# Writing out the prologue's order for every engine, three transpositions for k's maximum, and idle products in TensorE's waits

## The chip, the cores and the metric

The kernel runs on one core of a Trainium2 chip. The metric is the device time of one execution in microseconds (us), lower is better; 854.16 us is the median of three runs before the change. A core has a matrix engine (TensorE; PE in the rows, and PEld for its weight loads), a vector engine (VectorE, DVE), an activation engine (ScalarE, ACT), a general one (GpSimd, POOL) and a queue that issues the transfers (SyncE, SP). Each works through its own list of instructions in order and waits on semaphores for the others.

## The reference, cut to what matters

A linear attention (q softmaxed along the head dimension, k along the sequence), then two MLPs over all 2304 tokens, all in float32:

```python
# q, k, v: (4, 8, 576, 64)
q_s = exp(q - max(q, axis=-1)); q_s /= sum(q_s, axis=-1) + 1e-9
k_s = exp(k - max(k, axis=2));  k_s /= sum(k_s, axis=2) + 1e-9
kv  = einsum('bhsd,bhse->bhde', k_s, v)
x   = einsum('bhsd,bhde->bhse', q_s, kv)     # -> (2304, 512)
h   = x @ w_in;  x2  = (h - tanh(h)) @ w_out          # d_ff 2048
h2  = x2 @ w2_in; out = (max(h2,0) + log1p(exp(-|h2|))) @ w2_out
```

The inputs arrive as float64 bits; the kernel takes the float32 parts of the weights out of them itself.

## The kernel before

The 2304 tokens are cut into five blocks (512, 256, 512, 512, 512). For each block and each of four head pairs `hp`, `kv_task` makes the kv matrix of a batch and `x_task` makes the attention's output x, transposed, split into a high and a low float32r part (`xh`, `xl`). For each block and each of 16 steps `f`, `hidden` makes a tile h of the hidden layer with 12 products of 128x512, `gate` makes h - tanh(h) and splits it into `gh` and `gl`, and `mid_out` adds 12 products to the four output tiles x. The products of step n stand behind `hidden` of step n + 2. The second MLP follows when the first is done.

The weights come as 64-bit words. `w_task(p)` loads two steps' worth, and `convert` and `parts` turn each into a high and a low part: an ACT pass into `top` (L137), a DVE pass that joins it with the lower bits (L139), an ACT cast (L147, the high part), a DVE subtraction (L148, the low part). A tile i then holds the parts of w_in, a tile o those of w_out.

The prologue is the work before the first `hidden`: batch 0's four `kv_task`, block 0's four `x_task` and `w_task(0)`. Each is a generator. A string `order` says whose next part is recorded; a part holds the work of several engines, and a scheduler then sets each engine's list. For one k: the load; a maximum over the six rows of each partition in three DVE passes (L281 to L283, tile m); a transposition on TensorE (pm, L290); its maximum (mx, L292); a second transposition that spreads it over the partitions (pb, L295); the subtraction (L297); the exponential on ACT (L298); 12 products with v (pk, L305), two to a pair of rows, which use half of the array each; the reciprocal of the sum (r, L309 and L310); two scaled copies into kv (L313). For one q: the maximum (qm, L342), the subtraction on POOL (L344), the exponential (L345), the sum and its reciprocal (qsum, L348 to L350), the scaling on POOL (qn, L352), four transpositions (pt, L363), a copy (qs, L383), the product with kv (px, L388), and xh (L390) and xl (L391). The products of float32 tiles show as two rows each, the transpositions as one.

The eight PSUM banks have tags: two `h`, four `acc`, two `a`. The list `wide` hands the banks to the prologue's 20 tiles, from its end; its first entry, h0, goes to the last tile, px of head pair 3, and the first `hidden` needs h0 too.

All loads are issued by SP: k of all four head pairs, then q, then v, then the weights.

Of the kernel before, what the change touches and what calls it, by code (L numbers as in the profile page):

```python
# [9 lines left out]
F32 = mybir.dt.float32  # L10
# [11 lines left out]
def linear_attention_two_mlps(  # L22
# [32 lines left out]
    P = 128  # L55
# [62 lines left out]

    turn = itertools.count()

    def convert(raw, tops=None):

        words = raw.rearrange("p (f two) -> p f two", two=2)
        low, n = words[:, :, 0], words.shape[1]
        h3 = raw.bitcast(BF16).rearrange("p (f four) -> p f four", four=4)[:, :, 2]
        if tops:  # L130
            at_ = next(turn)
            top = tops[at_ % 2] if n > DM else tops[at_ // 2 % 2][:, at_ % 2 * DM :][:, :n]
        else:
# [9 lines left out]
        return f32(low)  # L143

# [12 lines left out]
    def w_task(p):  # L157
# [3 lines left out]
        for w, at_, pool_of in (("i", IN_AT, in_pool), ("o", OUT_AT, lambda _: weights_out)):  # L161
# [13 lines left out]
        yield  # L175
        yield
        if p:
            yield
            yield
        made = []  # L180
        for w, pool in (("i", in_pool(p)), ("o", weights_out)):
            made.append(pool.tile([P, 2, 2, DM], F32R, tag=f"{w}{p}", name=f"{w}0_{f}"))
        for k in range(2):
            wi[f + k] = tuple(made[0][:, n, k].rearrange("p (c f) -> p c f", c=NC) for n in range(2))
            wo[0, f + k] = tuple(made[1][:, n, k] for n in range(2))
        for k in range(2):

            for n, (t, raw) in enumerate(zip(made, raws)):
                if len(raw) == 2:
                    parts([part[:, k] for part in (t[:, 0], t[:, 1])], convert(raw[k], tops))  # L190
                elif k == n:
                    parts([part.rearrange("p k f -> p (k f)") for part in (t[:, 0], t[:, 1])], convert(raw[0], tops))
            yield
# [63 lines left out]
    def kv_task(b, hp, pool, bufs, lag=False):  # L257
# [15 lines left out]
        nc.gpsimd.memset(vt[:, :, :, D:], 1.0)  # L273
        m1 = pool.tile([KP, 2, D], F32, tag="m1", name=f"m1{nm}", bufs=bufs)
        if pool is att:

            m3 = vt[:, : KJ // 2, :, :D].rearrange("p j h d -> p h j d")
        else:
            load_v(vt)
            m3 = pool.tile([KP, 2, KJ // 2, D], F32, tag="m3", name=f"m3{nm}", bufs=2)  # L280
        nc.vector.tensor_tensor(m3, kt[:, :, : KJ // 2], kt[:, :, KJ // 2 :], op=ALU.max)  # L281
        nc.vector.tensor_tensor(m1, m3[:, :, 0], m3[:, :, 1], op=ALU.max)
        nc.vector.tensor_tensor(m1, m1, m3[:, :, 2], op=ALU.max)  # L283
        if pool is att:
            load_v(vt)
        yield
# [16 lines left out]
        for j in range(KJ):  # L303
            for h in range(2):
                nc.tensor.matmul(  # L305
                    pk[h * D : (h + 1) * D, : D + 2], kt[:, h, j], vt[:, j, h], start=j == 0, stop=j == KJ - 1
                )
        r = pool.tile([P, 1], F32, tag="r", name=f"r{nm}", bufs=bufs)
        nc.vector.tensor_scalar(r, pk[:, D : D + 1], 1e-9, None, op0=ALU.add)  # L309
        nc.vector.reciprocal(r, r)  # L310
        for h in range(2):
            d = slice(h * D, (h + 1) * D)
            nc.scalar.mul(kv[b % 2, hp][d, d], pk[d, :D], r[d])  # L313
# [8 lines left out]
    def x_task(i, hp, pool, bufs, lag=False):  # L322
# [39 lines left out]
        for j in range(J):  # L362
            nc.tensor.transpose(pt[:, j * P : (j + 1) * P], qn[:, j].rearrange("p h d -> p (h d)"), ident)  # L363
        if i == NB - 1:

# [15 lines left out]
        else:  # L381
# [206 lines left out]
    def advance():  # L588
        for t in list(running):
            if next(t, "end") == "end":  # L590
                running.remove(t)
# [39 lines left out]
    tasks |= {f"x{hp}": x_task(0, hp, pro, NHP) for hp in range(NHP)}  # L631
    tasks["w"] = w_task(0)
    order = """k0 k1 k2 k3 x0 x1 x2 x3 k0 k1 k2 k3 w k0 k1 k2 k3 x0 k0 x1 k1 x2 k2 x3 k3 x0 k0 x1 k1 x2 k2 x3 k3 x0 x1 w w x2 x3 x0 x1 x2 x3 w w"""
    for n, name in enumerate(order.split()):
        next(tasks[name], None)
        if n == 7:
            constants()
    assert all(next(t, None) is None for t in tasks.values())
    pro_stack.close()
# [7 lines left out]
    for n in range(min(starts), NB * NF - 2):  # L647
# [128 lines left out]
```

## Time and profile before

| | before |
|---|---|
| median of 3 runs (851.07 to 855.46) | 854.16 us |
| the profiled execution | 854.06 us, span 852.2 us |
| PE busy | 827.4 us, 97% |
| DVE, ACT, POOL busy | 496.4, 396.9, 28.2 us |
| chain that ended last, by engine | PE 82%, DMA 7%, DVE 5%, ACT 3% |

The profile is of one execution, and its span runs from the first to the last instruction; the execution's time is 1.9 us longer. PE's busy time counts a product from its start to its modelled end, so neighbours overlap. An idle time is put down to the instruction that ended it last. The column PEclk is the granted clock as a share of 2.4 GHz where the trace holds a record of it, and 1.00 where it holds none; the first record lies at 24.3 us.

### The profile page before, as it was taken

To read this page: it belongs to the slowest core of one execution; us is meant where nothing else is said; L and a number is where in the kernel's file an instruction comes from. 1 tells how busy PE (TensorE), PEld (TensorE's weight loads), DVE (VectorE), ACT (ScalarE), POOL (GpSimd) and SP (SyncE) were. 2 spreads that over 40 slices of the span, in tenths; PEclk is the share of its full clock that TensorE was granted. 3 is DMA by queue.
4 is the path that set the end of the run, shared out by engine and by line. 5 is a ranking of instruction groups with operands and counts; after the bars stand their busy time and mean duration, and the time that the engine had idled before them with its cause. 6 is when DMAs were issued, how large, how long until landed. Compare 5 with 4: busy or idle time off the path is not lost.

```text
span 852.2 us, 11605 instructions
## 1 busy us (share of the span) xinstructions
PE 827.4 (97%) x4348; PEld 711.2 (83%) x4348; DVE 496.4 (58%) x860; ACT 396.9 (47%) x628; POOL 28.2 (3%) x46
## 2 busy tenths in 40 slices
PE   4899999999999999999999999999999999999998
PEld 3677788987888888888888898899898898988986
DVE  7598998888764344444786543456633454634433
ACT  3796766566643232323756432344432443423322
POOL 5000000000000000010010000011000010000000
PEclk9899999999999999999999999999999999999999
DMA  9948677667710010022462644346544444544422
GB/s 253 318 152 253 207 234 263 200 200 250 243 58 13 11 51 13 13 74 70 165 243 89 200 115 126 112 120 197 185 124 112 117 121 121 186 124 111 116 58 75
DMA packets 86904, 121.32 MB, mean 142 GB/s; under 512 B 24640, under 2 KB 51264, under 8 KB 86848
## 3 DMA queue, kind: packets, MB, share of 16 engines
q1 hardware_dynamic: 86848, 120.57, 46.0%
q8 instruction: 35, 0.57, 0.3%
q14 instruction: 21, 0.17, 0.1%
HBM read 96.43 MB, written 24.12 MB: 141 GB/s over the span
## 4 chain that ended last, share of the span: by engine, by line
PE 82%; DMA 7%; DVE 5%; ACT 3%; issue 1%; SPq 1%; POOL 0%; ACTq 0%; DVEq 0%
PE h L406 17%; PE one L501 12%; PE o L572 8%; PE o L573 8%; PE o L571 8%; PE x L433 6%; PE x L434 6%; PE x L435 6%; PE seven L501 6%; DMA rawi<-in_moe_w_in_dram 4%; PE two L501 3%; PE px L388 1%; DMA x2d<-x2s 1%; PE pk L305 1%; PE pt L363 1%
## 5 line engine op out<-in xcount | busy, mean ns | idle before, releaser
L406 PE MATMUL h<-xh,i 128*128 128x512 f32 (+1 forms) x640 | 200.2, 379 | 3.5 <-DVE xl L391 3.5
L406 PEld LDWEIGHTS h<-xh,i 128*128 128x128 f32 x640 | 118.2, 190 | 25.3 <-DVE xl L391 4.3
L433 PE MATMUL x<-gh,o 128*128 128x512 f32 (+1 forms) x320 | 118.1, 369 | 2.2 <-DVE x2s L442 1.3
L406 PE MATMUL h<-xl,i 128*128 128x512 f32 (+1 forms) x320 | 119.0, 372 | 0.0
L434 PE MATMUL x<-gl,o 128*128 128x512 f32 (+1 forms) x320 | 118.0, 369 | 0.0
L435 PE MATMUL x<-gh,o 128*128 128x512 f32 (+1 forms) x320 | 117.9, 368 | 0.0
L501 PE MATMUL one<-xf,wf 128*128 128x384 f32 x576 | 116.8, 337 | 0.4 <-ACT u L516 0.4
L572 PE MATMUL o<-o,gh 128*128 128x512 f32 x288 | 113.7, 395 | 0.0
L573 PE MATMUL o<-o,gh 128*128 128x512 f32 x288 | 113.7, 395 | 0.0
L571 PE MATMUL o<-o,gl 128*128 128x512 f32 x288 | 112.3, 390 | 0.0
L501 PEld LDWEIGHTS one<-xf,wf 128*128 128x128 f32 x576 | 103.1, 188 | 7.0 <-ACT u L516 0.8
L416 DVE TENSOR_TENSOR g<-h,g 128x512 f32<-128x512 f32 (+1 forms) x80 | 50.6, 634 | 66.0 <-ACT g L415 65.8
L415 ACT ACTIVATE g<-h 128x512 f32<-128x512 f32 (+1 forms) x80 | 45.3, 566 | 85.7 <-PE h L406 85.4
L516 ACT COPY u<-one 128x384 f32<-128x384 f32 x72 | 34.4, 478 | 107.7 <-PE one L501 107.7
L521 DVE TENSOR_TENSOR hh<-seven,u 128x384 f32<-128x384 f32 x48 | 26.6, 554 | 86.0 <-ACT u L516 86.0
L433 PEld LDWEIGHTS x<-gh,o 128*128 128x128 f32 x320 | 60.3, 189 | 12.7 <-DVE x2s L442 1.5
L406 PEld LDWEIGHTS h<-xl,i 128*128 128x128 f32 x320 | 61.1, 191 | 9.5
L434 PEld LDWEIGHTS x<-gl,o 128*128 128x128 f32 x320 | 60.4, 189 | 9.8
L435 PEld LDWEIGHTS x<-gh,o 128*128 128x128 f32 x320 | 60.3, 189 | 9.9
L417 ACT CAST gh<-g 128x512 fp32r<-128x512 f32 (+1 forms) x80 | 46.6, 582 | 44.2 <-DVE g L416 44.1
L418 DVE TENSOR_TENSOR gl<-g,gh 128x512 fp32r<-128x512 f32 (+1 forms) x80 | 51.1, 639 | 25.1 <-ACT gh L417 24.4
L573 PEld LDWEIGHTS o<-o,gh 128*128 128x128 f32 x288 | 54.0, 187 | 11.9
(100 smaller groups left out, 1106.5 us busy)
## 6 DMA issues: line engine op xcount, KB each, us to landing
wf<-forms SPq DMA_DIRECT2D x168, 256.0 KB, 2.7
rawo<-in_moe_w_out_dram SPq DMA_DIRECT2D x32, 511.8 KB, 5.1
rawi<-in_moe_w_in_dram SPq DMA_DIRECT2D x32, 511.0 KB, 5.5
forms<-stage SPq DMA_DIRECT2D x24, 512.0 KB, 3.0
k<-in_k_dram SPq DMA_DIRECT2D x16, 288.0 KB, 3.9
v<-in_v_dram SPq DMA_DIRECT2D x32, 144.0 KB, 3.4
out_dram<-ot SPq DMA_DIRECT2D x18, 256.0 KB, 2.7
x2d<-x2s SPq DMA_DIRECT2D x16, 256.0 KB, 2.4
```

The costliest lines, as they stand in the source:

```text
L406: nc.tensor.matmul(p, w[:, c], x[:, c, :n], start=at == 0, stop=at == 3 * NC - 1)
L415: tanh[0] = nc.scalar.activation(g, h, AF.Tanh)
L416: nc.vector.tensor_tensor(g, h, g, op=ALU.subtract)
L417: nc.scalar.copy(gh, g)
L418: nc.vector.tensor_tensor(gl, g, f32(gh), op=ALU.subtract)
L433: nc.tensor.matmul(a, ol[:, s], gh, start=first, stop=False)
L434: nc.tensor.matmul(a, oh[:, s], gl, start=False, stop=False)
L435: nc.tensor.matmul(a, oh[:, s], gh, start=False, stop=last)
L501: nc.tensor.matmul(a, w[:, wp, c], x[:, xp, c], start=first and at == 0, stop=at == 5, skip_group_check=True)
L571: nc.tensor.matmul(a, gl[:, c], oh, start=first, stop=False)
L572: nc.tensor.matmul(a, gh[:, c], ol, start=False, stop=False)
L573: nc.tensor.matmul(a, gh[:, c], oh, start=False, stop=last)
```

## The change

1. The parts of the tasks are cut finer (`yield FINE`). Outside the prologue `advance` runs over the fine cuts, so the parts there stay as they were. `convert` and `parts` are joined into `steps_of`, which stops between its four passes; `w_task(0)` goes by them, first both halves of w_in, then both of w_out (before: w_in and w_out of the first half, then of the second).
2. A new string `order` names every fine part, and `in_order` makes each recorded instruction follow the one before it on its engine, so that the recorded order is the engine's order. What follows the prologue on ACT and DVE is held behind the prologue's last instruction on either.
3. The loads of q stand between those of k, and v of head pair 0 ahead of k of head pair 3.
4. In the prologue the three DVE passes for k's maximum become one (L299: 6 rows to 3); three transpositions (L314) and a maximum over 288 columns (L317, before 96) do the rest. Later k tasks keep the three passes.
5. A number in `order` stands for so many products of the identity with itself (128 columns, float32) into a bank that nobody reads (`idle`, in the bank of h1): 32 in all, six groups of 4 and one of 8, and two of the fours stand next to each other.
6. `wide` hands h0 to px of head pair 0 and to pk of head pair 3, h1 to none, and the last tile, px of head pair 3, gets an `acc` bank.

```diff
-    def convert(raw, tops=None):
+    def steps_of(raw, out=None, tops=None):
...
         nc.scalar.activation(upper, h3, AF.Copy, scale=2.0)
+        yield FINE
...
+        if out:
+            yield FINE
+            nc.scalar.copy(out[0], f32(low))
+            yield FINE
+            nc.vector.tensor_tensor(out[1], f32(low), f32(out[0]), op=ALU.subtract)
...
+        if p == 0:
+            for t, raw in zip(made, raws):
+                for k in range(2):
+                    yield from steps_of(raw[k], [part[:, k] for part in (t[:, 0], t[:, 1])], tops)
+                    yield FINE
+            return
...
-        nc.vector.tensor_tensor(m3, kt[:, :, : KJ // 2], kt[:, :, KJ // 2 :], op=ALU.max)
-        nc.vector.tensor_tensor(m1, m3[:, :, 0], m3[:, :, 1], op=ALU.max)
-        nc.vector.tensor_tensor(m1, m1, m3[:, :, 2], op=ALU.max)
+        nc.vector.tensor_tensor(
+            m3.rearrange("p j h d -> p h j d"), kt[:, :, : KJ // 2], kt[:, :, KJ // 2 :], op=ALU.max
+        )
         if pool is att:
+            nc.vector.tensor_tensor(m1, m3[:, 0], m3[:, 1], op=ALU.max)
+            nc.vector.tensor_tensor(m1, m1, m3[:, 2], op=ALU.max)
...
+            most = [m1]
+        else:
+            most = [m3[:, j] for j in range(KJ // 2)]
...
-        nc.tensor.transpose(pm[:, :KP], m1.rearrange("p h d -> p (h d)"), ident[:KP, :KP])
+        for j, of in enumerate(most):
+            nc.tensor.transpose(pm[:, j * KP : (j + 1) * KP], of.rearrange("p h d -> p (h d)"), ident[:KP, :KP])
+        yield FINE
         mx = pool.tile([P, 1], F32, tag="mx", name=f"mx{nm}", bufs=bufs)
-        nc.vector.tensor_reduce(mx, pm[:, :KP], axis=AX, op=ALU.max)
+        nc.vector.tensor_reduce(mx, pm[:, : len(most) * KP], axis=AX, op=ALU.max)
...
-    wide += ["h0", "acc", "a", "acc", "h1", "acc", "a", "acc"] * 2 + ["h0", "acc", "a", "acc"]
+    wide += ["acc", "a", "acc", "h0", "acc", "a", "acc"] * 2 + ["acc", "a", "acc", "acc", "a", "acc"]
...
+    def in_order():
...
+        for ins in traced[start:]:
+            if ins.engine in newest:
+                tc.add_manual_dep(ins, newest[ins.engine].name, ...)
+            newest[ins.engine] = ins
...
+            for _ in range(int(name)):
+                nc.tensor.matmul(idle[:, :P], ident, ident, start=True, stop=True)
...
-    order = """k0 k1 k2 k3 x0 x1 x2 x3 k0 k1 k2 k3 w k0 k1 k2 k3 x0 k0 x1 k1 x2 k2 x3 k3 x0 k0 x1 ... w w"""
+    order = """k0 q0 k1 q1 k2 q2 k0 k3 q3 k1 k2 k3 w k0 k0 q0 4 k0 q0 k1 k0 q0 k0 k1 k1 k0 q1 k1 8 k2 ... w w w w"""
+    behind = [newest[nc.scalar.engine], newest[nc.vector.engine]]
+    with tc.issue_after(behind[0]), tc.issue_after(behind[1]):
...
-            advance()
+            for ins in behind:
+                early.enter_context(tc.issue_after(ins))
+            advance()
```

How the change moves rows, at three places. The names are those of the tiles, with the head pair or step behind them. First the head of PE's list, before:

```order
L290 MATMUL pm_0_180<-ident,m_0_139 128x96
L290 MATMUL pm_1_184<-ident,m_1_148 128x96
L290 MATMUL pm_2_188<-ident,m_2_157 128x96
L290 MATMUL pm_3_192<-ident,m_3_166 128x96
L295 MATMUL pb_0_200<-ident,mx_0_182 96x128
L295 MATMUL pb_1_208<-ident,mx_1_186 96x128
L295 MATMUL pb_2_216<-ident,mx_2_190 96x128
L295 MATMUL pb_3_224<-ident,mx_3_194 96x128
L305 MATMUL pk_0_234<-v_0_137,k_0_99 64x66 x12
```

and after:

```order
L314 MATMUL pm_0_163<-ident,m_0_161 128x96 x3
L695 MATMUL idle<-ident 128x128 x4
L320 MATMUL pb_0_178<-ident,mx_0_173 96x128
L314 MATMUL pm_1_182<-ident,m_1_176 128x96 x3
L320 MATMUL pb_1_191<-ident,mx_1_186 96x128
L695 MATMUL idle<-ident 128x128 x8
L314 MATMUL pm_2_209<-ident,m_2_201 128x96 x3
L332 MATMUL pk_0_213<-v_0_112,k_0_100 64x66 x12
L320 MATMUL pb_2_239<-ident,mx_2_232 96x128
```

One head pair's maximum now runs to its spreading (pb) before the next one starts, with three transpositions each, and the first 12 idle products stand between them.

The end of the prologue on PE, before:

```order
L363 MATMUL pt_2_348<-ident,qn_2_280 128x128 x4
L363 MATMUL pt_3_355<-ident,qn_3_304 128x128 x2
L305 MATMUL pk_3_306<-v_3_164,k_3_105 64x66 x11
L363 MATMUL pt_3_355<-ident,qn_3_304 128x128 x2
L388 MATMUL px_0_362<-qs_0_329,kv_121 128x512
L388 MATMUL px_1_366<-qs_1_336,kv_123 128x512
L388 MATMUL px_2_370<-qs_2_353,kv_125 128x512
L388 MATMUL px_3_374<-qs_3_360,kv_127 128x512
L406 MATMUL h_0_421<-xh_97,i_0_338 128x512
L406 MATMUL h_0_421<-xl_98,i_0_338 128x512
```

and after:

```order
L695 MATMUL idle<-ident 128x128 x8
L395 MATMUL pt_2_341<-ident,qn_2_335 128x128 x4
L421 MATMUL px_1_351<-qs_1_328,kv_126 128x512
L332 MATMUL pk_3_355<-v_3_150,k_3_116 64x66 x12
L421 MATMUL px_2_372<-qs_2_353,kv_128 128x512
L395 MATMUL pt_3_379<-ident,qn_3_369 128x128 x4
L695 MATMUL idle<-ident 128x128 x4
L421 MATMUL px_3_394<-qs_3_391,kv_130 128x512
L695 MATMUL idle<-ident 128x128 x4
L441 MATMUL h_0_450<-xh_97,i_0_337 128x512
```

The products px of head pairs 1 and 2 now stand ahead of the transpositions of head pair 3, and 16 idle products stand in this piece, the last four between px of head pair 3 and the first product of h_0.

ACT from the last xh to the first tanh (L415, after: L450), before:

```order
L137 ACTIVATE top_93<-rawi_1_174 128x512
L137 ACTIVATE top_92<-rawo_0_177 128x512
L390 ACTIVATE xh_97<-px_3_374 128x512
L137 ACTIVATE top_93<-rawo_0_177 128x512
L147 CAST o_0_339<-rawo_0_177 128x512
L147 CAST i_0_338<-rawi_1_174 128x512
L137 ACTIVATE top_92<-rawi_2_396 128x512
L147 CAST o_0_339<-rawo_0_177 128x512
L137 ACTIVATE top_92<-rawi_3_397 128x512
L415 ACTIVATE g_0_434<-h_0_421 128x512
```

and after:

```order
L424 ACTIVATE xh_97<-px_2_372 128x512
L424 ACTIVATE xh_97<-px_3_394 128x512
L138 ACTIVATE top_92<-rawi_1_155 128x512
L147 CAST i_0_337<-rawi_1_155 128x512
L138 ACTIVATE top_93<-rawo_0_158 128x512 x2
L138 ACTIVATE top_92<-rawi_2_425 128x512
L147 CAST o_0_338<-rawo_0_158 128x512 x2
L147 CAST i_2_438<-rawi_2_425 128x512
L450 ACTIVATE g_0_463<-h_0_450 128x512
```

Before, the passes of `w_task(0)` began ahead of the last xh, and a pass of the next pair of steps (rawi_3) stood ahead of the tanh; now every pass of `w_task(0)` but the first tile's, and both of rawi_2's, stand between the last xh and the tanh, and rawi_3's stands behind it.

## Rows read from the trace of the kernel before

**Rows 1.** Waits of PE from 32.3 us to the end: total us, times, longest:

```profile
PE h L406 <- DVE xl L391: 3.5, 1, 3.5
...
PE pm L290 <- DVE m L283: 1.3, 2, 0.8
```

**Rows 2.** Timeline of PE: start us, us, what, [idle before and releaser]:

```profile
19.10 1.58 PE L305 MATMUL pk<-v,k 96*64 96x66 f32 x22
...
21.86 2.18 PE L363 MATMUL pt<-ident,qn 128*128 128x128 f32 x9
23.97 1.06 PE L305 MATMUL pk<-v,k 96*64 96x66 f32 x22
...
25.23 3.60 PE L388 MATMUL px<-qs,kv 128*128 128x512 f32 x8
32.33 0.80 PE L406 MATMUL h<-xh,i 128*128 128x512 f32 x1 [3.49 <-DVE xl L391]
...
34.62 1.06 PE L406 MATMUL h<-xh,i 128*128 128x512 f32 x2
...
35.90 1.06 PE L406 MATMUL h<-xh,i 128*128 128x512 f32 x2
...
38.94 0.61 PE L406 MATMUL h<-xh,i 128*128 128x512 f32 x2
...
39.62 0.61 PE L406 MATMUL h<-xh,i 128*128 128x512 f32 x2
...
43.24 0.39 PE L433 MATMUL x<-gh,o 128*128 128x512 f32 x1
```

**Rows 3.** Stretches of 2 us: busy us (and count) by engine, PEclk, DMA share, GB/s:

```profile
30.00:32.00 2.00, 0.00 (x0) 0.00 (x0) 1.68 (x4) 2.00 (x5) 0.00 (x0) 0.78 0.85 230
...
34.00:36.00 2.00, 2.00 (x6) 1.54 (x6) 1.88 (x4) 1.49 (x3) 0.00 (x0) 0.50 1.01 405
```

**Rows 4.** Timeline of DVE:

```profile
4.12 0.56 DVE L281 TENSOR_TENSOR m<-k 96x384 f32<-96x384 f32 x1 [4.12 <-DMA k<-in_k_dram]
...
10.16 0.74 DVE L292 TENSOR_REDUCE mx<-pm 128x1 f32<-128x96 f32 x4
10.95 1.81 DVE L297 TENSOR_TENSOR k<-k,pb 96x768 f32<-96x768 f32 x2
...
15.59 0.67 DVE L348 TENSOR_REDUCE qsum<-q 128x8 f32<-128x512 f32 x1
...
18.56 0.97 DVE L349 TENSOR_SCALAR qsum<-qsum 128x8 f32<-128x8 f32 x2
...
31.59 0.68 DVE L391 SCALAR_TENSOR_TENSOR xl<-px,xh 128x512 fp32r<-128x512 f32 x1
...
38.48 0.69 DVE L416 TENSOR_TENSOR g<-h,g 128x512 f32<-128x512 f32 x1 [2.60 <-ACT g L415]
```

**Rows 5.** Timeline of POOL:

```profile
17.39 2.04 POOL L352 TENSOR_TENSOR qn<-q,qsum 128x512 f32<-128x512 f32 x2 [1.45 <-DVE r L309]
```

**Rows 6.** Timeline of ACT:

```profile
30.18 0.77 ACT L137 ACTIVATE top<-rawo 128x512 f16<-128x512 bf16 x1
...
31.89 0.66 ACT L147 CAST o<-rawo 128x512 fp32r<-128x512 f32 x1
...
37.85 0.60 ACT L415 ACTIVATE g<-h 128x512 f32<-128x512 f32 x1 [2.36 <-PE h L406]
```

**Rows 7.** Line L111 between 13.5 and 14.3 us: its issues and their landing:

```profile
L111 SPq DMA_DIRECT2D rawi<-in_moe_w_in_dram x2: 623/672/722, 13.2 to 13.9; - x2
...
DMA to landing us min/median/max: 5.3/5.7/6.1
```

**Rows 8.** Stretches of 10 us, columns as in rows 3:

```profile
40.00:50.00 10.00, 10.00 (x46) 8.29 (x45) 8.97 (x12) 8.94 (x12) 0.00 (x0) 1.00 0.74 263
50.00:60.00 10.00, 10.00 (x45) 8.27 (x45) 9.44 (x11) 8.81 (x11) 0.00 (x0) 1.00 0.50 162
60.00:70.00 10.00, 9.51 (x63) 7.33 (x62) 9.90 (x20) 8.02 (x10) 0.12 (x1) 1.00 0.41 120
```

More of the change, by code (lines that the diff above doesn't have):

```diff
@@ L1 @@
 import itertools
-from contextlib import ExitStack
+from contextlib import ExitStack, contextmanager
 import concourse.bass as bass
@@ L142, in convert @@
             nc.vector.scalar_tensor_tensor(low, top, 0xFFFF0000, low, op0=ALU.bitwise_and, op1=ALU.bitwise_or)
-        return f32(low)
+        if out:
[3 more added lines that the diff above has]
+            nc.vector.tensor_tensor(out[1], f32(low), f32(out[0]), op=ALU.subtract)
+    def convert(raw, out=None, tops=None):
+        for _ in steps_of(raw, out, tops):
+            pass
+        return f32(raw.rearrange("p (f two) -> p f two", two=2)[:, :, 0])
     def parts(out, x):
@@ L174, in w_task @@
                     load_out(each[k], w1_out, f + k)
-        yield
-        yield
         if p:
-            yield
-            yield
+            for _ in range(4):
+                yield
+        else:
+            yield FINE
         made = []
@@ L189, in w_task @@
                 if len(raw) == 2:
[L190 removed]
+                    convert(raw[k], [part[:, k] for part in (t[:, 0], t[:, 1])], tops)
                 elif k == n:
[L192 removed]
+                    convert(raw[0], [part.rearrange("p k f -> p (k f)") for part in (t[:, 0], t[:, 1])], tops)
             yield
@@ L589, in advance @@
         for t in list(running):
-            if next(t, "end") == "end":
+            at_ = FINE
+            while at_ == FINE:
+                at_ = next(t, "end")
+            if at_ == "end":
                 running.remove(t)
@@ L628, in linear_attention_two_mlps @@
     x_tiles(0)
-    wide += ["h0", "acc", "a", "acc", "h1", "acc", "a", "acc"] * 2 + ["h0", "acc", "a", "acc"]
+    wide += ["acc", "a", "acc", "h0", "acc", "a", "acc"] * 2 + ["acc", "a", "acc", "acc", "a", "acc"]
     tasks = {f"k{hp}": kv_task(0, hp, pro, NHP) for hp in range(NHP)}
-    tasks |= {f"x{hp}": x_task(0, hp, pro, NHP) for hp in range(NHP)}
+    tasks |= {f"q{hp}": x_task(0, hp, pro, NHP) for hp in range(NHP)}
     tasks["w"] = w_task(0)
-    order = """k0 k1 k2 k3 x0 x1 x2 x3 k0 k1 k2 k3 w k0 k1 k2 k3 x0 k0 x1 k1 x2 k2 x3 k3 x0 k0 x1 k1 x2 k2 x3 k3 x0 x1 w w x2 x3 x0 x1 x2 x3 w w"""
@@ L634, in linear_attention_two_mlps @@
-    for n, name in enumerate(order.split()):
[L635 to L638, printed above, removed]
+    idle = ps.tile([P, 512], F32, tag="h1", name="idle", bufs=1)
+    newest = {}
+    @contextmanager
+    def in_order():
+        traced = nc.cur_bb.bb.instructions
+        begin = traced[-1] if len(traced) else None
+        yield
+        start = next((n + 1 for n in reversed(range(len(traced))) if traced[n] is begin), 0)
+        for ins in traced[start:]:
+            if ins.engine in newest:
+                tc.add_manual_dep(
+                    ins,
+                    newest[ins.engine].name,
+                    mybir.DependencyInfo(mybir.DependencyClass.NoSync, mybir.DependencyReason.DATA),
+                    reason="in_order",
+                )
+            newest[ins.engine] = ins
@@ new lines, in take @@
+    def take(name):
+        if name.isdigit():
+            for _ in range(int(name)):
+                nc.tensor.matmul(idle[:, :P], ident, ident, start=True, stop=True)
+        else:
+            next(tasks[name], None)
+    order = """k0 q0 k1 q1 k2 q2 k0 k3 q3 k1 k2 k3 w k0 k0 q0 4 k0 q0 k1 k0 q0 k0 k1 k1 k0 q1 k1 8 k2 q1 q2 k1 q1
+        q2 k2 k0 q0 q2 k1 k2 q0 k0 k2 q3 k0 q0 k2 q3 q0 k1 k3 k2 q1 q0 q3 k3 k2 q0 k1 q1 k3 k1 4 k2 q2 q1 k2
+        k3 4 q1 k3 4 q2 w q0 q2 k3 q3 q1 q2 k3 w q3 q1 q2 k3 w q1 q3 4 k3 w q3 q2 q3 4 q3 q2 q3 w w w w"""
@@ L639, in linear_attention_two_mlps @@
+    for n, name in enumerate(order.split()):
+        with in_order():
+            take(name)
+            if n == 7:
+                constants()
+    behind = [newest[nc.scalar.engine], newest[nc.vector.engine]]
+    with tc.issue_after(behind[0]), tc.issue_after(behind[1]):
+        for t in tasks.values():
+            assert all(at_ == FINE for at_ in t)
     pro_stack.close()
@@ L656, in linear_attention_two_mlps @@
             x_tiles(blk + 1)
-        advance()
+        with ExitStack() as early:
+            if n < 0:
+                for ins in behind:
+                    early.enter_context(tc.issue_after(ins))
+            advance()
         while n >= -2 and len(gated) < min(n + 3, len(steps)):
```

20 lines of the change are left out of this document (17 added, 3 removed).

## The prediction

> **What bounds the kernel now.** I read the page's busy times first (PE 97% of the span), then PE's waits, its timeline over the first 45 us, and the other engines' timelines there. After 32.3 us PE hardly stops: [rows 1] show that the wait for xl, 3.5 us, ends at the first `hidden`, and that the only other waits of the first MLP's early part are two on DVE, 1.3 us together. So what comes before 32.33 us [rows 2] is nearly pure head: an earlier first `hidden` moves the whole chain, as long as DVE and ACT follow. They have little to spare: from 40 to 70 us DVE is busy 8.97 to 9.90 of each 10 us and ACT 8.02 to 8.94 [rows 8].
>
> The second cost is the clock. The steps of the same 22 rows of pk take 1.58 us at 19.1 us and 1.06 us at 24.0 us, though the column shows 1.00 for both [rows 2]: the prologue starts at the lower level (1.2 GHz) and PE rises after it has worked almost without a break from 18.5 us on. Then it waits 3.49 us for xl, and the granted clock is 0.78 and 0.50 [rows 3]: three products of `hidden` take 1.28 us (34.62 to 35.90) and later 0.68 us (38.94 to 39.62) [rows 2], 0.427 and 0.227 us each. The 36 products of h_0 to h_2 take 10.91 us from 32.33 to 43.24; at 0.227 they would take 8.17. The lost clock costs 2.7 us.
>
> **What the change costs, part by part.** I laid the new lists side by side and gave each row the step that its form has in the trace, each starting when its engine is free and its inputs are there.
>
> *Prices.* Three DVE passes of k's maximum become the first of them, 0.56 us [rows 4]. The maximum over 288 columns is not in the trace: four over 96 take 0.74 us, near 0.17 each, one over 512 some 0.60 (0.67 with its tail) [rows 4]; 288 lies between, and I take 0.36. Three transpositions cost 0.16 each at the lower level (9 of 128 columns take 2.18 with the last one's tail, 0.22 a step, three quarters of that), 0.08 at the upper. An idle product is not in the trace either. px is a float32 product of 512 columns: eight rows, two to a product, 3.60 us at the upper level, 0.43 a row and 0.86 a product [rows 2]; a quarter of the columns is 0.215, and 0.43 at the lower level. The other bound is the transposition, 0.11 to 0.22. I take the product's price: 32 of them are 6.9 us at the upper level, 13.7 at the lower, 3.5 at the least.
>
> *Loads.* k of head pair 0 stays first in SP's list, and its maximum starts at 4.12 [rows 4]. k of head pair 1 stands one load later (some 1.2 us) and is needed only behind the first subtraction. k of head pair 3, the most delayed, has about 4 us to spare by my walk. The first two weights keep their place behind the same bytes: they land near 18.5 and 20.0 us (issued at 13.2 and 13.9, 5.3 and 6.1 us on the way [rows 7]); the walk uses them at 20.3 and 27.3. The load order is at nothing; were q's bytes to hold k of head pair 1 beyond 8 us, each us would be one on the path.
>
> *The walk, first half (lower clock).* m_0 at 4.1, pm_0 4.7, four idle products until 6.9, pb_0, subtraction 7.4 to 8.3 (0.87 each by the two in 1.81 [rows 4]), mx_1 to 8.65, pb_1 8.9, eight idle products from 9.1 to 12.5, pm_2 to 13.0, pk_0 to 14.35, so r_0 on DVE at 14.6. The eight hold pm_2 back by some 2 us: m_2 is ready at 10.2. From 9.1 us on PE has no gap, so I let its clock rise between 12.5 and 16 us.
>
> *Second half (upper clock).* DVE now runs without a break: r_0 0.3, qm_3 0.6, subtraction 0.87, m_3 0.5, qsum_1 with its two small passes 1.05, r_1 0.3, mx_3 0.36, r_2 0.3, qsum_2 1.05, which is 5.3 us, and 0.3 for a wait explained next: 20.2. qn_2 on POOL takes 1.0 (two in 2.04 [rows 5]): 21.3, where the eight idle products end as well. PE then does pt_2 0.43, px_1 0.86, pk_3 0.70, px_2 0.86, pt_3 0.43, to 24.7. The next four idle products (0.86) lie under the copy qs_3; px_3 ends at 26.5; four more until 27.4, then h_0. Those four cost nothing, since h_1 needs the second half of w_in, split at 30.1; without that cover they would cost 0.86.
>
> The wait: at 18.56 two small passes of DVE take 0.97 us together, and end with POOL's second scaling (two from 17.39, 2.04 long, to 19.43) [rows 4, 5]. A DVE pass with an input from SBUF alone stood there until POOL was done. In the new order m_1 and m_3 start beside a POOL subtraction, about 0.5 and 0.3 us. By the Trainium skill, GPSIMD Engine Reference, section 8, Key points, GpSimd shares its SBUF interfaces with VectorE and contends with passes that read two SBUF inputs or run in a 2-port mode; the trace agrees with its one case of 0.8 us, and if every such pass in the prologue met POOL the sum would be some 3 us worse.
>
> *Correction.* The same walk over the old lists puts the first `hidden` at 31.2; the trace has 32.33. I add 1.1: **h_0 at 28.5, 3.8 us earlier.** With the clock held (PE is never idle for more than about 0.7 us from 9 us on), h_2 could start at 28.5 + 24 x 0.227 = 33.9; before, it starts 12 products ahead of 43.24, at 40.5. That would be 6.6 us.
>
> *Given back.* h_2 uses h_0's bank and must wait for DVE's h - tanh(h) of step 0. Its tanh stood at 37.85 after 2.36 us of idle ACT [rows 6]. Now eight ACT passes stand between the last xh (27.3) and the tanh: four into top at 0.63 a step and four casts at 0.56 (0.77 and 0.66 with their tails [rows 6]), and one wait of 0.9 for DVE's joining pass: tanh at 32.95, DVE's subtraction 33.8 to 34.4, h_2 at 34.6, with the correction 35.7. The lead at h_2 is 40.5 - 35.7 = 4.8 us. DVE's subtraction, 38.48 before [rows 4], is at 34.9, 3.6 us earlier, but with one 0.6 us pass more behind it, and the lists have no DVE idle there to lose. Moved bank: the last px no longer holds h0, so h_0 does not wait for the last xl (31.59 + 0.68 before [rows 4]); that is in the 28.5. Of the 1.3 us of PE's later waits on DVE I expect half back: 0.6.
>
> **Sum:** 4.8 + 0.6 = 5.4 us off the profiled execution's 854.06, which lies 0.1 below the median of 854.16: 848.7 us.
>
> **The rivals.**
>
> *The clock rises late or falls again.* For: none of PE's early work before 18.5 us raised it, and the price doubles every PE step. Against: PE has no gap after 9.1 us in the new list, while before it stood from 16.4 to 18.5. If it rises only at 20 the walk ends 1.6 us later, at 24.2 (as before) 3.8 later: 850 to 853. The same holds if it falls before h_0.
>
> *The idle products run at the lower level throughout, and the kernel is slower.* One mechanism: 13.7 us of them in an ordered list, each in front of real work. With no rise before h_0 the walk ends at 38.3, 39.4 corrected, 7 us behind, and h_0 to h_1 still run slow: about 859.5. It decides from where the clock rises after about 27 us; earlier, something is left. The Trainium skill, TensorE: Matmul & The Clock Gate, Part 1, says that the throttled state is the default and activity releases it; the rows at 24 us agree, and by that rule the filled list rises.
>
> *DVE and ACT take it back.* They are nearly full from 40 to 70 us [rows 8], so what PE leads beyond DVE's 3.6 us turns into waits: 854.06 - 3.0 = 851. Against: DVE idled 2.60 us ahead of 38.48 [rows 4], which goes away.
>
> *The order does nothing.* If real latencies make each strictly ordered engine wait for another's late row, xh_3 stays near 31 us and only the clock's 2.7 us could be won, less the wait at h_2: 853 to 854.5.
>
> **How the numbers follow.** The forecast (clock up by 17 us, lead of 4 to 8 us) has 0.60, late clock 0.17, DVE and ACT 0.10, no effect 0.07, slower 0.06. The likeliest's own range is 846.0 (correction not needed, idle products at the transposition's price) to 850.3. The range to 854.0 takes in the late clock, the backlog and part of no effect: 846.0 to 854.0. Within 0.5%, 4.3 us, is about what a measurement of this kernel can't tell from no change; the bound is 849.9. Of the forecast's cases nearly all lie below it: faster 0.60, same 0.33, slower 0.07.
>
> **What would show it.** h_0 between 27 and 30 us; products of `hidden` at 0.227 us from the first on, PEclk 1.00 at 28 to 36 us; a wait of h_2 on DVE of 1 to 2 us; the steps of pk at the upper level from pk_1 or pk_2 on; tanh of h_0 33 to 35 us. I am wrong if PE's early steps stay slow past 20 us, if DVE passes beside POOL last over 0.9 us more than a few times, or if the waits between 40 and 140 us grow beyond 3 us.

## The result and the profile after

The changed kernel takes 844.70 us (median of 6 executions, 843.91 to 846.46) against 852.08 us for the kernel before on the same chip (six executions, 849.73 to 855.46, three of them those of the table of before): ratio 0.9912, 95% interval 0.9888 to 0.9936. That is 7.4 us faster (5.5 to 9.5 by the interval) where I forecast 5.4, and below the range's lower end of 846.0. The profiled execution is the slowest of the six, 846.46 us with a span of 844.7, against 854.06 and 852.2.

The page of the changed kernel, busy times:

```profile
PE 830.8 (98%) x4420; PEld 716.3 (85%) x4420; DVE 495.6 (59%) x852; ACT 396.3 (47%) x628; POOL 28.6 (3%) x46
```

PE is busy 3.4 us longer than before, idle products included, in a span 7.5 us shorter. Its timeline:

```profile
9.39 3.41 PE L695 MATMUL idle<-ident 128*128 128x128 f32 x16
...
12.98 0.92 PE L332 MATMUL pk<-v,k 96*64 96x66 f32 x24
...
20.38 1.95 PE L695 MATMUL idle<-ident 128*128 128x128 f32 x16
...
28.47 0.48 PE L441 MATMUL h<-xh,i 128*128 128x512 f32 x1
...
29.02 0.63 PE L441 MATMUL h<-xh,i 128*128 128x512 f32 x2
...
35.86 0.50 PE L441 MATMUL h<-xh,i 128*128 128x512 f32 x1 [1.29 <-DVE g L451]
```

The first `hidden` starts at 28.47 us, against 32.33 [rows 2]. The eight idle products (16 rows) take 3.41 us at 9.4 us and 1.95 at 20.4, and pk_0 runs at 0.92 us for 24 rows already: PE is at the lower level at 9.4 us and at the upper one by 13.0. h_2 waits 1.29 us for DVE's h - tanh(h) and starts at 35.86, 4.7 us earlier than before (40.5, twelve products ahead of 43.24 [rows 2]).

ACT ahead of the first tanh, then DVE's subtraction behind it, the counterparts of [rows 6] and [rows 4]:

```profile
30.04 0.65 ACT L147 CAST i<-rawi 128x512 fp32r<-128x512 f32 x1 [0.76 <-DVE rawi L141]
...
34.20 0.60 ACT L450 ACTIVATE g<-h 128x512 f32<-128x512 f32 x1
```

```profile
35.12 0.68 DVE L451 TENSOR_TENSOR g<-h,g 128x512 f32<-128x512 f32 x1
```

The stretches that answer to [rows 3] and [rows 8]:

```profile
34.00:36.00 2.00, 0.71 (x4) 0.29 (x3) 2.00 (x4) 2.00 (x5) 0.00 (x0) 1.00 1.02 381
40.00:50.00 10.00, 10.00 (x46) 8.28 (x45) 9.74 (x12) 9.33 (x11) 0.00 (x0) 1.00 0.91 307
50.00:60.00 10.00, 9.88 (x46) 7.50 (x44) 10.00 (x17) 9.62 (x12) 0.00 (x0) 1.00 0.51 144
```

The clock stays at 1.00 through h_2's wait. From 40 to 60 us DVE is idle 0.26 us, where it was idle 1.59 before [rows 8]: it has lost its slack.

So the head is as predicted. The rest of this pair of profiles, 7.5 - 4.7 = 2.8 us, comes behind h_2, where PE waits less. PE's waits from 44 to 470 us, before (the two on m, 1.3 us, stand in [rows 1]):

```profile
PE x L433 <- DVE x2s L442: 1.3, 1, 1.3
...
PE x L433 <- ACT x2s L440: 0.9, 1, 0.9
PE px L388 <- ACT kv L313: 0.4, 1, 0.4
PE px L388 <- ACT qs L383: 0.4, 1, 0.4
```

and after:

```profile
PE x L468 <- DVE x2s L477: 0.6, 1, 0.6
PE pk L332 <- DMA rawo<-in_moe_w_out_dram: 0.5, 1, 0.5
PE px L421 <- ACT kv L342: 0.4, 1, 0.4
```

4.3 us against 1.5. The experiments ask why.

### The profile page after: what moved, and what is told of

Its sections match the earlier page's. It is cut to its first block, busy times and chain, and to the rows that moved or that the text cites. A ratio compares the mean times of both kernels' runs of the same rounds, so it can differ in the third digit from the quotient of the medians.

```text
span 844.7 us, 11758 instructions
## 1 busy us (share of the span) xinstructions
PE 830.8 (98%) x4420; PEld 716.3 (85%) x4420; DVE 495.6 (59%) x852; ACT 396.3 (47%) x628; POOL 28.6 (3%) x46
## 4 chain that ended last, share of the span: by engine, by line
PE 84%; DMA 5%; DVE 4%; ACT 3%; SPq 2%; issue 1%; DVEq 0%; ACTq 0%
PE h L441 18%; PE one L536 12%; PE o L607 8%; PE o L608 8%; PE o L606 8%; PE x L468 6%; PE x L470 6%; PE x L469 6%; PE seven L536 6%; PE two L536 3%; DMA rawi<-in_moe_w_in_dram 2%; PE pk L332 1%; PE px L421 1%; DMA v<-in_v_dram 1%; DMA k<-in_k_dram 1%
## 5 line engine op out<-in xcount | busy, mean ns | idle before, releaser
L450 ACT ACTIVATE g<-h 128x512 f32<-128x512 f32 (+1 forms) x80 | 45.3, 566 | 68.6 <-PE h L441 68.1
L468 PEld LDWEIGHTS x<-gh,o 128*128 128x128 f32 x320 | 60.3, 189 | 10.9 <-DVE x2s L477 0.8
```

The source lines that it names most:

```text
L450: tanh[0] = nc.scalar.activation(g, h, AF.Tanh)
L468: nc.tensor.matmul(a, ol[:, s], gh, start=first, stop=False)
```

## The experiments

The changed prologue also changes what the scheduler does behind it: 149 of 4052 places in PE's later list differ, 129 of 595 in ACT's, 228 of 804 in DVE's and 24 of 368 in SP's, so the later loads change places too. To keep the two apart I wrote the order behind the prologue out, so that an edit of the prologue leaves it alone. `table` holds the order, instruction by instruction:

```diff
+    def fixed_order(since, table):
...
+            for a, b in itertools.pairwise(line):
+                tc.add_manual_dep(own[b], own[a].name, ..., reason="fixed_order")
...
     pro_stack.close()
+    prologue_end = nc.cur_bb.bb.instructions[-1]
...
+    fixed_order(prologue_end, TABLE)
```

All runs but free_bank and old_start_idle have it; in those two the scheduler set the order behind the prologue anew. The ratio is to the kernel before on the same chip; the clock is the mean granted clock of each execution, lowest and highest. The kernel before, in 45 executions beside these runs, had 0.992 to 1.000 and took 850.3 to 860.0 us.

| run | median us (n) | ratio [95%] | span profiled | clock |
|---|---|---|---|---|
| new_start_old_order | 848.36 (6) | 0.9927 [0.9901, 0.9954] | 846.2 | 1.000 |
| old_start_new_order | 852.39 (12) | 0.9972 [0.9950, 0.9994] | 850.4 | 0.995 to 1.000 |
| old_start_idle | 852.17 (12) | 0.9974 [0.9956, 0.9993] | 851.8 | 0.997 to 0.999 |
| no_idle | 848.89 (6) | 0.9925 [0.9895, 0.9954] | 843.2 | 0.997 to 1.000 |
| after_again | 846.15 (4) | 0.9897 [0.9879, 0.9914] | 844.9 | 0.999 to 1.000 |
| late_pe | 848.11 (6) | 0.9924 [0.9906, 0.9941] | 846.0 | 0.993 to 1.000 |
| free_bank | 845.14 (4) | 0.9884 [0.9864, 0.9904] | 844.7 | 0.999 to 1.000 |
| three_passes | 846.26 (4) | 0.9896 [0.9878, 0.9914] | 844.5 | 0.999 to 1.000 |
| early_weights | 846.28 (5) | 0.9896 [0.9875, 0.9916] | 844.5 | 0.999 to 1.000 |
| own_bank | 845.85 (6) | 0.9900 [0.9880, 0.9920] | 843.9 | 0.994 to 1.000 |
| first_idle_only | 846.40 (6) | 0.9902 [0.9881, 0.9922] | 846.7 | 0.995 to 1.000 |
| k_loads_first | 848.37 (6) | 0.9925 [0.9906, 0.9944] | 846.6 | 0.999 to 1.000 |

**The order behind the prologue: new_start_old_order and old_start_new_order.** Each kernel got the other's table, for all five engines:

```diff
-    4052: """0+37 39 37+2 40+32 73+24 98+13 72 111+3 97 114+8 137+4 122 141+2 123+11 143+5 134+2 148+13 164+10
+    4052: """0+72 73+24 98+24 137+5 72 142+5 97 147+14 122+12 164+2 134+2 166+22 136 161+2 202+2 163 204+17 18
```

(the start of PE's part: each entry is the place of an instruction as recorded, or a first place + so many).

> The changed prologue, with everything behind the prologue in the order of the kernel before on each engine (the two kernels' lists differ there: 149 of 4052 places on PE, 129 of 595 on ACT, 228 of 804 on DVE). The lead at h_2 is 4.7 us in the changed kernel and 7.6 us at 236 us, because PE's waits behind h_2 are 4.8 us before and 1.8 to 2.0 us after. Theory A (ACT and DVE reach each tile earlier, so the waits shrink whatever the order): waits behind h_2 at about 2 us, time 844 to 846. Theory B (the scheduler set another order behind the prologue, and that takes the waits away): lead of 4.7 at h_2 as after, waits behind it near 4.8, time 847 to 848.

> The reverse: the prologue of the kernel before, with everything behind it in the changed kernel's order. Theory A (an earlier start of ACT and DVE): waits behind h_2 near 4.8 us, time 851 to 853, no difference from before. Theory B (the order): waits behind h_2 near 2 us with no lead at h_2, time 848.5 to 849.5.

PE's waits from 44 to 470 us, new_start_old_order:

```profile
PE pm L314 <- DVE m L304: 2.0, 2, 1.4
PE x L468 <- DVE x2s L477: 1.2, 1, 1.2
```

and old_start_new_order:

```profile
PE x L433 <- DVE x2s L442: 1.1, 1, 1.1
PE px L388 <- ACT kv L313: 0.9, 1, 0.9
PE x L434 <- DVE gl L418: 0.7, 1, 0.7
```

Four corners: 4.3 us (both old), 3.2 (new start, old order), 2.7 (old start, new order), 1.5 (both new). Neither theory alone gives that. But sums of waits of one execution are good to about 1.5 us only (after_again, below), and the corners differ by 1.1 to 1.7. The spans are better: 852.2, 846.2, 850.4, 844.7 (844.9 in after_again), which put the order at 1.3 to 1.8 us. With the old start the new order has the ratio 0.9972, its interval below 1 (0.5 to 4.3 us). With the new start the old order has 0.9927 against 0.9912 and 0.9897 for the changed kernel, with overlapping intervals; its six executions, 847.83 to 848.70, all lie above the ten of the changed kernel and after_again, 843.91 to 846.64, which ran on other chips. The order accounts for a part; how much the earlier start adds, these sums can't tell.

Wait by wait it is clearer. The waits on m are the order's: 1.3 us before, 2.0 in new_start_old_order, none in the changed kernel and in old_start_new_order. The waits of before for qs and for ACT's x2s, 1.3 us, stand in no other profile behind its prologue, with the old start or the new; ahead of that x2s ACT had waited 1.76 us for a transfer:

```profile
203.88 0.38 ACT L440 ACTIVATE x2s<-x 128x256 f32<-128x256 f32 x1 [1.76 <-DMA x2d<-x2s]
```

So 1.3 of the 2.8 us may belong to that one execution of the kernel before.

new_start_old_order also shows what the new start is worth if the order stays: h_2 starts at 35.99 us, 4.5 earlier than before, but pm of the third k task behind the prologue at 86.11 us against 89.69, only 3.6 earlier. DVE's h - tanh(h) of step 0 starts at 34.65 there, 3.8 us earlier than before [rows 4]. What PE led beyond DVE was taken back.

What the order does shows in DVE's waits from 36 to 76 us, before:

```profile
DVE g L416 <- ACT g L415: 2.6, 1, 2.6
DVE rawo L139 <- ACT top L137: 2.4, 2, 1.8
```

(the first hangs on the start: it is 3.4 us in old_start_new_order too) and in new_start_old_order, where ACT's timeline tells the rest:

```profile
DVE rawo L141 <- ACT top L138: 3.0, 2, 2.4
```

```profile
66.48 0.38 ACT L416 COPY qs<-pt 128x256 f32<-128x256 f32 x1 [1.79 <-PE pt L395]
...
68.53 1.38 ACT L138 ACTIVATE top<-rawo 128x1024 f16<-128x1024 bf16 x1 [1.15 <-DMA rawo<-in_moe_w_out_dram]
```

In the old order ACT stands 1.79 us for a transposition and then 1.15 for a weight load, DVE's joining pass stands behind it, and the maximum of the next k, on which pm waits, stands behind that. In the changed kernel ACT waits longer for the transposition (two waits, 6.0 us), but DVE's list has other work there, and its waits on top are 0.2 us.

**How exact that is: after_again.** No instruction moved against the changed kernel.

> The changed kernel once more, with its own order behind the prologue written out (no instruction moves): the measure for the three runs beside it. 844 to 846, granted clock 0.999 to 1.000 in every execution, PE's waits behind h_2 about 2 us.

```profile
PE pk L332 <- DMA v<-in_v_dram: 2.3, 1, 2.3
PE x L468 <- DVE x2s L477: 0.6, 1, 0.6
```

PE's waits in the same view are 2.9 us, not 1.5: one load of v came 2.3 us late in this execution, and the prologue 0.7 us earlier. Sums of waits of one execution are good to about 1.5 us, spans better (844.9 and 844.7).

**PE later and earlier at h_2: late_pe, free_bank, own_bank, early_weights.**

```diff
-        k3 4 q1 k3 4 q2 w ... w q3 q2 q3 4 q3 q2 q3 w w w w"""
+        k3 4 q1 k3 4 q2 w ... w q3 q2 q3 16 q3 q2 q3 w w w w"""
```

> The changed kernel with 16 idle products ahead of h_0 in place of 4, so that h_0 starts 2.6 us later; ACT's and DVE's lists stay. h_2 waits 1.3 us for DVE in the changed kernel, and the tanh of h_0 is held by eight ACT passes, not by h_0. Theory A (what PE has as a lead is taken back by waits on ACT and DVE): h_2 later by about 1.3 us, PE's waits behind it smaller by up to as much, time 0 to 1 us above the changed kernel. Theory B (the waits depend on the order alone): the whole 1.3 us or more at the end, waits behind h_2 still about 2 us.

h_2 no longer waits, the first x product starts at 39.12 us against 38.09 in after_again, and the span is 846.0 against 844.9. What PE loses ahead of h_2 beyond its wait stays lost: 1.0 us there, 1.1 at the end; the medians, on the same chip, differ by 2.0. In time Theory B holds. The other sign decides nothing: the waits behind h_2 are 1.6 us against 2.9, as Theory A has it, but 2.3 of the 2.9 are after_again's late load of v.

In the other direction, a bank of tag a for h_2. free_bank leaves the order behind the prologue to the scheduler, which sets another one (hence the first words of its expectation); own_bank has the changed kernel's.

```diff
     def psum_h(i, f):
+        if i == 0 and f == 2:
+            return ps.tile([P, 512], F32, tag="a", name=f"h{i}_{f}", bufs=2)
```

> Placeholder of order: the changed kernel with h_2 of the first block in a bank of its own kind, so that it doesn't wait for DVE's h - tanh(h) of step 0. Theory A (ACT and DVE set the pace): h_2 starts 1.2 us earlier, but the products behind it wait longer, time within 0.5 us of the changed kernel. Theory B: PE keeps the 1.2 us, time 843 to 844.

> free_bank again, with the order behind the prologue as in the changed kernel, which free_bank's scheduler had set otherwise. h_2 then waits for i_2 alone, 0.7 us in place of 1.3. Theory A (PE keeps an earlier h_2): PE's last product about 0.6 us earlier than the changed kernel's 840.5 to 840.7. Theory B (ACT and DVE take it back): waits behind h_2 longer by as much, 840.5 again.

h_2 waits 0.7 us, for i_2, in both. The spans are 844.7 and 843.9; the ratios can't be told from after_again's. Whether PE keeps the 0.6 us stays open: the difference is smaller than what separates two executions, and in own_bank h_2 starts at 35.90, no earlier than in the changed kernel, because h_0 came at 29.12.

early_weights takes on the whole wait:

```diff
-        ... k3 w q3 q2 q3 4 q3 q2 q3 w w w w"""
+        ... k3 w q3 q2 q3 w q3 q2 w q3 w w"""
```

with the two casts of o_0 on ACT and their subtractions on DVE put behind the tanh of h_0 in the table.

> The changed kernel with three edits at h_2's wait: ACT's pass into top for the second half of w_in and DVE's joining pass stand ahead of the last xh and xl (ACT stands still there for 0.7 us), the two casts of w_out's first tile and their DVE subtractions stand behind the tanh of h_0, and the last four idle products are out. By the rows of the changed kernel the tanh of h_0 comes at 32.3 to 32.8 in place of 34.2, g_0 on DVE ends near 33.6, i_2 is ready at 33.0, so h_2 follows h_1 without a wait, at 33.7 to 34.2 in place of 35.2 to 35.9. Theory A (ACT's and DVE's total work sets the pace behind it): h_2's 1.5 us comes back as waits behind it, time as the changed kernel, within 0.5 us. Theory B (PE keeps what h_2 gains): PE's last product 1 to 2 us earlier, ratio to the kernel before near 0.988. The clock could fall where the four products are out; the granted clock of the executions tells.

PE at h_2 and at the first k task of the next block:

```profile
34.56 0.50 PE L441 MATMUL h<-xh,i 128*128 128x512 f32 x1 [0.83 <-DVE g L451]
...
55.62 0.30 PE L314 MATMUL pm<-ident,m 96*128 96x96 f32 x1 [1.46 <-DVE m L304]
```

and there in the changed kernel:

```profile
55.58 0.30 PE L314 MATMUL pm<-ident,m 96*128 96x96 f32 x1
```

h_2 starts 1.30 us earlier, though it still waits 0.83, and 21 us later pm starts at the same time to 0.04 us, after a wait of 1.46 on DVE, which is busy 10.00 of 10 us from 50 to 60 and starts the last pass of that maximum at 55.28 (55.24 in the changed kernel). Theory A, for this direction: the changed kernel has brought PE to where DVE sets the pace at 55 us. More lead of PE is worth nothing there; less is lost (late_pe).

**The idle products: old_start_idle, no_idle, first_idle_only.**

```diff
+    idle = ps.tile([P, 512], F32, tag="h1", name="idle", bufs=1)
+    for _ in range(16):
+        nc.tensor.matmul(idle[:, :P], ident, ident, start=True, stop=True)
     pro_stack.close()
```

> The kernel before with 16 products of the identity on PE between the last px and h_0, which fill its 3.5 us wait, and nothing else. Clock theory (h_0 to h_2 take 10.9 us in place of 8.2 because PE idles ahead of them): products of h_0 at 0.23 us from the first on, 2.4 to 2.7 us earlier at h_2, and 849.5 in all if the later waits stay. Rival (ACT and DVE set the pace there): PE's waits behind h_2 grow by as much, time 851 to 853. Rival (the products themselves run past xl and hold h_0 back): h_0 up to 3 us later.

The clock stays up ahead of the first x product, which starts at 41.63, 1.6 us earlier than before [rows 2], though h_0 starts at 33.31, 1.0 us later: the 36 products take 8.3 us in place of 10.9, so the lost clock, 2.7 us in the prediction, is 2.6. Then, in the profiled execution, PE waits longer at the second block's end, and the clock falls behind that wait:

```profile
140.42 0.39 PE L433 MATMUL x<-gh,o 128*128 128x256 f32 x1 [2.68 <-DVE x2s L442]
```

```profile
138.00:142.00 4.00, 1.58 (x12) 1.52 (x13) 3.16 (x10) 2.80 (x8) 0.00 (x0) 1.00 0.66 225
142.00:146.00 4.00, 4.00 (x23) 4.00 (x23) 3.15 (x9) 1.05 (x3) 0.00 (x0) 0.57 0.81 262
```

so that the span is only 0.4 us shorter. The ratio, 0.9974, is 2.2 us over many executions, interval 0.6 to 3.8, and the median of 852.17 us lies where the first rival has it. It doesn't price the clock by itself: the order behind the prologue changed with the 16 products (ACT's list differs from its fifth row behind the start of h_0 on, DVE's from its sixth), and the longer wait may come from that.

```diff
-    order = """... k0 k0 q0 4 k0 q0 ... q1 k1 8 k2 ... k1 4 k2 ... k3 4 q1 k3 4 q2 ... q3 4 k3 ... q3 4 q3 q2 q3 ..."""
+    order = """... k0 k0 q0 k0 q0 ... q1 k1 k2 ... k1 k2 ... k3 q1 k3 q2 ... q3 k3 ... q3 1 q3 q2 q3 ..."""
```

(no_idle; first_idle_only keeps the first 4 and the 8.)

> The changed kernel with all idle products out but one, and the order behind the prologue as it is in the changed kernel. Clock theory: PE stands at the lower level until after 17 us, its steps there take twice as long, h_0 starts 0.5 to 2 us later and parts of h_0 to h_2 run at 0.43 us a product: 846 to 849. Rival (PE's own list is not what sets h_0, so the idle products change nothing but the last four's place): h_0 0 to 0.9 us earlier, 844 to 845.

> The changed kernel with the first 12 idle products and one ahead of h_0; 19 in the second half are out. Without any, PE's clock rose between 14.5 and 18 us too, h_0 came 0.9 us earlier and the profiled execution ended 1.5 us earlier, but other executions stood at a mean granted clock of 0.997 and took 849. Theory A (the first twelve raise the clock, the later ones hold it): executions spread as without any, 845 to 849. Theory B (only the early ones matter): mean granted clock 0.999 to 1.000 in all executions, time 0.5 to 1.5 us below the changed kernel.

PE's timeline in no_idle:

```profile
10.55 2.12 PE L332 MATMUL pk<-v,k 96*64 96x66 f32 x24
...
14.50 1.81 PE L332 MATMUL pk<-v,k 96*64 96x66 f32 x24
...
18.28 0.92 PE L332 MATMUL pk<-v,k 96*64 96x66 f32 x24
...
21.88 0.66 PE L395 MATMUL pt<-ident,qn 128*128 128x128 f32 x4 [1.98 <-POOL qn L384]
...
27.57 0.48 PE L441 MATMUL h<-xh,i 128*128 128x512 f32 x1
```

Without idle products the clock rises too, some 5 us later (the first record of the granted clock, 1.00, lies at 17.8 us, in the changed kernel at 12.4), and h_0 starts 0.9 us earlier, as the rival has it; this execution, at a granted clock of 1.000, has the shortest span of all profiled ones, 843.2. But four of the six executions took 848.9 to 849.4, and the median is 848.89: ratio 0.9925, where the changed kernel has 0.9897 and 0.9912. In first_idle_only the profiled execution caught the falls, by stretches:

```profile
20.00:24.00 4.00, 2.75 (x20) 1.43 (x22) 2.97 (x7) 3.00 (x6) 2.38 (x2) 0.76 1.03 383
24.00:28.00 4.00, 3.27 (x24) 2.01 (x21) 1.62 (x5) 2.22 (x5) 0.00 (x0) 0.81 1.07 384
...
136.00:140.00 4.00, 2.96 (x17) 2.96 (x18) 2.71 (x8) 1.90 (x6) 0.00 (x0) 0.77 0.68 230
```

the first behind PE's wait of 1.76 us ahead of pt_2, the second behind one of 1.90 for x2s. So the later idle products don't raise the clock. That they keep it from falling in some executions is what the counts suggest: without them 5 of 12 executions have a mean granted clock below 0.999 (no_idle, first_idle_only), and 2 of the 42 with the new prologue and all of them (one in late_pe, one in own_bank). That they are worth anything in time is not shown: no_idle's and first_idle_only's intervals overlap the changed kernel's. What the 4 us between no_idle's executions are made of stays open: one at a mean granted clock of 1.000 took 849.26, and the mean knows nothing of the time ahead of the trace's first record.

The Trainium skill, TensorE: Matmul & The Clock Gate, Part 1, has activity release the throttled state; no_idle agrees, since the kernel's own products raised the clock there.

**k's maximum: three_passes.**

```diff
+        nc.vector.tensor_tensor(m1, m3[:, 0], m3[:, 1], op=ALU.max)
+        nc.vector.tensor_tensor(m1, m1, m3[:, 2], op=ALU.max)
+        most = [m1]
         if pool is att:
-            nc.vector.tensor_tensor(m1, m3[:, 0], m3[:, 1], op=ALU.max)
-            nc.vector.tensor_tensor(m1, m1, m3[:, 2], op=ALU.max)
             load_v(vt)
-            most = [m1]
-        else:
-            most = [m3[:, j] for j in range(KJ // 2)]
```

> The changed kernel with k's maximum by three DVE passes, one transposition and a maximum over 96 columns, as before, in the new order. By my prices DVE gets two passes of 0.35 to 0.5 us more for each head pair and saves 0.2 at mx: 2 to 3 us more on DVE, which the walk has without a break from 14.6 us on; of them some 1.5 to 2.5 reach xh and h_0: 846.5 to 848. Rival (the waits for loads and for POOL hide it): h_0 less than 0.7 us later, time within 0.5 us of the changed kernel.

```profile
6.69 0.57 DVE L300 TENSOR_TENSOR m<-k 96x384 f32<-96x384 f32 x1 [0.73 <-DMA k<-in_k_dram]
7.29 0.29 DVE L303 TENSOR_TENSOR m<-m 96x128 f32<-96x128 f32 x1
7.62 0.29 DVE L304 TENSOR_TENSOR m<-m,m 96x128 f32<-96x128 f32 x1
8.69 0.25 DVE L316 TENSOR_REDUCE mx<-pm 128x1 f32<-128x96 f32 x1
```

h_0 starts at 28.66, 0.2 us later than in the changed kernel's profile and 0.9 later than in after_again's, and the time is the same: 846.26 us against 846.15 in after_again, on the same chip. The two passes take 0.29 us each, not 0.35 to 0.5 (one of the eight, beside a POOL pass, 1.01), mx is 0.2 us shorter (0.25 against 0.46), and of what is left a part goes into waits that DVE has anyway: for k_1, 0.73 here and 1.27 in the changed kernel. No gain from part 4 of the change shows here.

**The order of the loads: k_loads_first.**

```diff
-    order = """k0 q0 k1 q1 k2 q2 k0 k3 q3 k1 k2 k3 w k0 ..."""
+    order = """k0 k1 k2 k3 q0 q1 q2 q3 k0 k1 k2 k3 w k0 ..."""
```

> The changed kernel with the loads in the order of before: k of the four head pairs, then q, then v. In the changed kernel k of head pair 1 landed at 7.25 us and DVE waited 1.3 us for it. My prediction has the order of the loads at nothing: h_0 within 0.3 us, time within 0.5 us. Rival A: k_1 comes 1 us earlier and with it the eight idle products and pk_0: h_0 0.5 to 1 us earlier. Rival B: q of head pair 0 comes 2 to 4 us later, POOL's and ACT's work on it with it, and h_0 1 to 2 us later.

DVE, then POOL:

```profile
8.45 0.69 DVE L371 TENSOR_REDUCE qm<-q 128x8 f32<-128x512 f32 x1 [3.99 <-DMA q<-in_q_dram]
9.05 0.45 DVE L317 TENSOR_REDUCE mx<-pm 128x1 f32<-128x288 f32 x1
9.42 1.26 DVE L299 TENSOR_TENSOR m<-k 96x384 f32<-96x384 f32 x1
```

```profile
9.22 1.04 POOL L374 TENSOR_TENSOR q<-q,qm 128x512 f32<-128x512 f32 x1 [4.72 <-DMA q<-in_q_dram]
```

qm_0 is second in DVE's written list, and with q behind four k it waits 3.99 us with mx_0 queued behind it. h_0 comes 2.2 us later and the span is 1.9 us longer; the median is 848.37 us where the three other runs on its chip have 845.85 to 846.40. Rival B: the loads' order, which I put at nothing, is worth about 2 us, because the new list needs q_0 at once.

## Why the prediction was off

The walk, with its correction of 1.1 us, held. h_0 at 28.5 (28.47; 27.81 in after_again, whose lists are the same), the tanh between 33 and 35 (34.20), h_2's wait of 1 to 2 us on DVE (1.29), h_2 at 35.7 (35.86), the lead there of 4.8 us (4.66) came out as worked out. The rise of the clock between 12.5 and 16 us came at the early edge: the eight idle products up to 12.8 us ran at the lower level, pk_0 at 13.0 at the upper. An idle product costs about 0.24 us at the upper level (1.95 for eight, with the last one's tail) and 0.43 at the lower (3.41 for eight), as priced. mx over 288 columns takes 0.46 with its tail, 0.10 more than I took. The last four idle products cost next to nothing, as said: in no_idle h_0 is 0.9 us earlier, and h_2, which waits 1.29 us there too, 0.3 us.

The step that failed is "Of the 1.3 us of PE's later waits on DVE I expect half back: 0.6". Behind h_2 the profiled pair gains 2.8 us, and after_again 2.0 (7.3 of span less the 5.3 by which its h_2, at 35.19, is ahead). Two things were wrong in the step. It counted only the two waits of [rows 1]; the waits for x2s, kv and qs behind them, another 3.0 us, stood in the same answer. And it took the order behind the prologue for unchanged. It is not: the scheduler sets it from what it sees ahead, and the new one alone is worth 1.3 to 1.8 us by the spans (old_start_new_order, new_start_old_order), by keeping DVE's joining pass from standing behind ACT's wait for a weight load. Had the order stayed, nothing would have come back on these waits: new_start_old_order, the step's own premise, has 2.0 us of waits on m in place of 1.3, and PE's lead has shrunk from 4.5 us to 3.6 at 86 us. Where the rest of the 2.8 us comes from stays open; 1.3 of it may be chance in the one profiled execution of the kernel before.

Not all of the miss is the sum's. The forecast was counted from 854.16 us, a median of three; with three more executions the same kernel stands at 852.08. So 2.1 of the 4.0 us between 848.7 and 844.70 are the base, and 2.0 the gain. The gain is above 5.4 in both measurements (5.5 to 9.5 us, and 7.3 to 10.3 in after_again), but its size is known to no better than 2 us.

A second slip stands beside the step: "the lists have no DVE idle there to lose". [rows 8] show 1.59 us of DVE idle from 40 to 60 us, and 1.33 of it went. That may be how PE's waits could shrink although PE's lead at h_2 (4.7 us) is larger than DVE's (38.48 to 35.12, 3.4 us); it is argued from the totals.

Three parts were mis-sized without touching the sum, since the walk took the new kernel as a whole: the loads, put at nothing, are worth 2 us to a list that asks for q_0 early; the shorter form of k's maximum, which the walk rests on, shows no gain; and the idle products, by which the walk raises the clock, were not needed for the rise, nor for an early h_0 (27.57 in no_idle).

None of the rivals came in the changed kernel. "DVE and ACT take it back" has the right mechanism: it is what new_start_old_order shows under the old order, and with the new one it begins where the change ends, as early_weights shows.

## What to carry to other kernels

A change ahead of a scheduled list changes that list too: compare the two orders far behind the edit, and transplant one into the other kernel before a later gain or loss is put down to the edit's own mechanism. Sum every wait of the bounding engine to the end of the run, not those of the stage in hand, and look at a second execution before a wait is booked as one that can be won. A forecast in microseconds also needs a base from more than three executions when they spread by 4 us. When a lead stops paying, look for the engine that reaches the same instruction at the same time in both kernels (pm at 55.58 and 55.62): that one is the next bound.

## What the runs showed of the hardware

The granted clock differs between executions of one and the same list: 0.992 to 1.000 for the kernel before, with 850.3 to 851.9 us in the four at 1.000 and 860.0 in the one at 0.992. In two profiles PE's waits of 1.76, 1.90 and 2.68 us were followed by stretches at a mean of 0.76, 0.77 and 0.57, so that such a wait cost twice. Length alone doesn't decide it: in after_again PE waited 2.32 us and the clock stayed at 1.00,

```profile
73.94 0.30 PE L332 MATMUL pk<-v,k 96*64 96x66 f32 x2 [2.32 <-DMA v<-in_v_dram]
```

```profile
74.00:78.00 4.00, 4.00 (x37) 3.17 (x38) 2.59 (x5) 1.34 (x3) 0.12 (x1) 1.00 1.08 332
```

and so it did behind the 1.98 us ahead of pt_2 in no_idle.

A DVE pass of 0.55 us took 1.26 us when it started beside a POOL pass (9.42 to 10.68, POOL until 10.26, k_loads_first): it ended 0.42 us after POOL did, as if most of its work had waited, which is what the prediction had read from [rows 4, 5]. Not every pass stands: a maximum of q at 10.43 us in the changed kernel took its usual 0.69 beside POOL's passes from 9.77 to 12.23.
